# Two chunks' down projections joined into one Strassen product, with the output projection of the second chunk moved into the first one's gate and up products

## The chip, the cores and the metric

The kernel runs on one core of one Trainium2 chip. The metric is the device time of one execution in microseconds; each kernel was run several times, on the same chip as runs of the kernel before. The time is 1.7 to 2.8 us longer than the span of the trace, which goes from the first to the last instruction.

## The reference

A pre-layernorm transformer block over 2048 rows of width 1024: a sliding, dilated attention (32 heads of 32, 8 keys at distance 0, 2, ..., 14), and a bilinear feed-forward part of width 3584. Weights and rows are bf16.

```python
x = A_x
h  = x + attention(layernorm(x), wqkv) @ wo      # attention over positions s, s-2, ..., s-14
g  = layernorm(h) @ w_gate                       # (2048, 1024) @ (1024, 3584)
u  = layernorm(h) @ w_up
h2 = h + (g * u) @ w_down                        # (2048, 3584) @ (3584, 1024)
```

## The kernel before

The 2048 rows go through in four chunks of 512. TensorE first makes q, k and v of all chunks, then for chunks 0 and 1 in turn: output projection, gate and up products (7 blocks of 8 groups of 8 matmuls), down projection (chunk 1's output projection stands ahead of chunk 0's down projection). Chunks 2 and 3 are done together by a loop over pairs of blocks at the end ("the pair loop"). The attention runs on VectorE as background work: a generator whose steps are emitted between the matmul groups.

```python
# weights come in through one queue (SP) into 7 buffers; retire() frees buffers and issues the next loads
def retire(n=1):
    state["live"] -= n
    pump()

# background work: a generator yields what a step costs; ("later", us) puts it off
class Background:
    def spend(self, us): self.credit -= us          # withholds steps worth so many us
    def step(self, us): ...                         # emits steps while there is credit

def load_qk(c):                                     # q and k of chunk c for the attention, 2.1 MB
    ...
    nc.gpsimd.dma_start(qD[:], qd[c].rearrange("c g d s -> (c g) d s"))
    nc.gpsimd.dma_start(kD[:], kd[c].rearrange("c g d s -> (c g) d s"))

def attention(c):
    ...                                             # logits, Exp on ScalarE, 8 products with v
    nc.gpsimd.dma_start(od[c].rearrange("c g d s -> (c g) d s"), oD[:])        # to DRAM
    for cp in range(4):                             # and back, transposed, one row tile each
        nc.gpsimd.dma_start(oT[:, :, cp, :], od[c][cp].rearrange("(hg hl) d s -> (hl d) hg s", hl=4))

def wo_ln2(c):                                      # output projection and second layernorm, chunks 0 and 1
    def norm(t):
        ln = normalize(hs[t], mv4, rs4, t)          # VectorE
        nc.sync.dma_start_transpose(lnT[:, :, bass.ts(t, 128)], ln[:])
    ...

def ffn1(c, lnT, at={}):                            # gate and up of one chunk
    for b in range(7):
        for j in range(4):
            mm_group(pg, wts["wg", c, b], j, lnT);  nc.scalar.copy(gs[:], pg[:])
            mm_group(pu, wts["wu", c, b], j, lnT);  nc.scalar.copy(us[:], pu[:])
            nc.vector.tensor_tensor(gs[:], gs[:], us[:], ALU.mult)
            abs_sum(c, b, j)                        # ScalarE: sums of |w|, for the scales of the f16 products
            ...
        retire(2)
# ... cut: qkv, the first layernorm, the down projections, the pair loop
```

The down projection of chunk 0 was plain (224 matmuls, into `acc`), that of chunk 1 one level of Strassen (seven products of blocks, with sums and differences of blocks as operands, in f16 with power-of-two scales that come from sums of absolute values). Three words for what follows: a *total* is a matmul with ones that adds such sums over the 128 partitions, a *scale* is the power of two that VectorE makes of the total, and a *seed* is ScalarE's scaled copy of one psum bank into another, to which TensorE then adds.

## Time and profile before

| what | value |
|---|---|
| time, median of 3 runs (range) | 777.07 us (776.86 to 777.39) |
| span of the trace, granted clock | 775.2 us, 1.00 |
| TensorE busy, matmuls | 769.3 us (99%), 3691 |
| VectorE, ScalarE, GpSimd busy | 605.3, 484.0, 142.1 us |
| waits of TensorE, all together | 2.8 us: 2.2 in the start, 0.6 in the pair loop |
| bytes moved by DMA | 134.38 MB |

### The profile page before, as it was taken

To read this page: it belongs to the slowest core of one execution; us is meant where nothing else is said; L and a number is where in the kernel's file an instruction comes from. 1 tells how busy PE (TensorE), PEld (TensorE's weight loads), DVE (VectorE), ACT (ScalarE), POOL (GpSimd) and SP (SyncE) were. 2 spreads that over 40 slices of the span, in tenths; PEclk is the share of its full clock that TensorE was granted. 3 is DMA by queue.
4 is the path that set the end of the run, shared out by engine and by line. 5 is a ranking of instruction groups with operands and counts; after the bars stand their busy time and mean duration, and the time that the engine had idled before them with its cause. 6 is when DMAs were issued, how large, how long until landed. Compare 5 with 4: busy or idle time off the path is not lost.

```text
span 775.2 us, 10420 instructions
## 1 busy us (share of the span) xinstructions
PE 769.3 (99%) x3691; PEld 353.5 (46%) x3691; DVE 605.3 (78%) x766; ACT 484.0 (62%) x1040; POOL 142.1 (18%) x152
## 2 busy tenths in 40 slices
PE   8999999999999999999999999999999999999998
PEld 6444444444444444444444444444444444444444
DVE  5639999999999989999979859985553444578863
ACT  4639564322866662965777899746677776788240
POOL 0000000200002000011000001008778687600000
PEclk9999999999999999999999999999999999999999
DMA  8998896997947964978445592644332423740001
GB/s 278 265 260 199 157 230 151 299 271 224 310 133 236 308 235 125 288 257 277 142 143 192 182 299 68 157 98 114 109 95 69 109 59 106 240 140 28 0 28 55
DMA packets 183716, 134.38 MB, mean 173 GB/s; under 512 B 81264, under 2 KB 176496, under 8 KB 181616
## 3 DMA queue, kind: packets, MB, share of 16 engines
q1 hardware_dynamic: 176912, 110.12, 50.9%
q0 software_dynamic: 3584, 22.02, 8.9%
q10 hardware_dynamic: 3168, 1.57, 0.8%
q8 instruction: 29, 0.48, 0.3%
q14 instruction: 23, 0.19, 0.1%
HBM read 104.86 MB, written 22.02 MB: 164 GB/s over the span
## 4 chain that ended last, share of the span: by engine, by line
PE 93%; DVE 3%; DMA 2%; ACT 1%; issue 0%; ACTq 0%; DVEq 0%
PE ps L411 20%; PE pg L411 12%; PE pu L411 12%; PE dx L807 6%; PE pz L700 6%; PE acc L646 6%; PE py L700 6%; PE px L700 6%; PE wo L532 4%; PE wo L852 4%; PE pv L700 3%; PE dy L807 3%; PE ex L807 2%; DMA lnT<-lnr 1%; DMA w_qkv<-in_A_wqkv_dram 1%; PE ps L372 1%
## 5 line engine op out<-in xcount | busy, mean ns | idle before, releaser
L411 PE MATMUL ps<-lnT,w_qkv 128*128 128x512 bf16 x736 | 159.5, 379 | 0.0
L411 PEld LDWEIGHTS <-w_qkv 128*128 128x128 bf16 x736 | 71.9, 98 | 86.2
L411 PE MATMUL pu<-lnT,w_wu 128*128 128x512 bf16 x448 | 105.8, 379 | 0.0
L411 PE MATMUL pg<-lnT,w_wg 128*128 128x512 bf16 x448 | 105.8, 379 | 0.0
L324 ACT CAST sg<-ps 128x512 bf16<-128x512 f32 x96 | 55.2, 585 | 52.3 <-PE ps L411 49.2
L451 DVE TENSOR_TENSOR prod<-qD,kD 128x4096 bf16<-128x4096 bf16 x32 | 72.4, 2285 | 12.8 <-DMA kD<-kd 12.7
L494 DVE TENSOR_TENSOR pv<-vD,at 128x4096 bf16<-128x4096 bf16 x32 | 72.5, 2285 | 0.3
L700 PEld LDWEIGHTS <-sw 128*128 128x128 f16 x448 | 43.8, 98 | 53.8 <-issue 1.2
L411 PEld LDWEIGHTS <-w_wu 128*128 128x128 bf16 x448 | 43.8, 98 | 52.9
L411 PEld LDWEIGHTS <-w_wg 128*128 128x128 bf16 x448 | 43.7, 98 | 52.8
L616 ACT CAST us<-pu 128x512 bf16<-128x512 f32 x56 | 33.0, 590 | 43.0 <-PE pu L411 41.8
L700 PE MATMUL px<-lnT,ws 128*128 128x512 bf16 x224 | 55.2, 379 | 0.0
L700 PEld LDWEIGHTS <-ws 128*128 128x128 f16 x336 | 32.9, 98 | 39.7
L506 POOL DMA_DIRECT2D od<-oD x4 | 2.2, 542 | 264.3 <-DVE oD L504 264.3
L646 PE MATMUL acc<-w_wd,gs 128*128 128x512 bf16 x224 | 48.5, 379 | 0.0
L681 POOL TENSOR_TENSOR sw<-ws 128x512 f16<-128x512 f16 x26 | 30.0, 1152 | 85.1 <-PE py L700 77.8
L611 ACT CAST gs<-pg 128x512 bf16<-128x512 f32 x56 | 32.6, 583 | 12.9 <-PE pg L411 10.6
L453 DVE TENSOR_TENSOR prod<-prod 128x4096 bf16<-128x4096 bf16 x16 | 36.6, 2289 | 0.4
L560 ACT ACTIVATE junkd<-w_wd 128x512 bf16<-128x512 bf16 x56 | 34.3, 613 | 0.0
L646 PEld LDWEIGHTS <-gs 128*128 128x128 bf16 x224 | 21.9, 98 | 26.4
L617 DVE TENSOR_TENSOR gs<-gs,us 128x512 bf16<-128x512 bf16 x56 | 23.5, 419 | 12.5 <-ACT us L616 12.5
L185 ACT ACTIVATE rs<-mv,eps 128x1 f32<-128x1 f32 (+1 forms) x21 | 6.2, 297 | 42.0 <-DVE mv L182 36.6
(321 smaller groups left out, 1391.5 us busy)
## 6 DMA issues: line engine op xcount, KB each, us to landing
w_wg<-in_B_w_gate_dram SPq DMA_DIRECT2D x14, 1024.0 KB, 6.7
w_wu<-in_B_w_up_dram SPq DMA_DIRECT2D x14, 1024.0 KB, 5.4
w_wd<-in_B_w_down_dram SPq DMA_DIRECT2D x8, 896.0 KB, 6.2
w_pair<-in_B_w_gate_dram SPq DMA_DIRECT2D x14, 512.0 KB, 4.0
w_pair<-in_B_w_up_dram SPq DMA_DIRECT2D x14, 512.0 KB, 5.2
w_wo<-in_A_wo_dram SPq DMA_DIRECT2D x6, 1024.0 KB, 6.2
w_qkv<-in_A_wqkv_dram SPq DMA_DIRECT2D x5, 1024.0 KB, 11.0
kd<-sg SPq DMA_DIRECT2D x32, 144.0 KB, 3.3
```

The costliest lines, as they stand in the source:

```text
L324: nc.scalar.copy(sg[:, HB:HB + TC], ps[:])
L411: nc.tensor.matmul(ps[:], lhsT=wt[:, ko, bass.ts(j, 128)], rhs=rhs[:, ko, :], start=(ko == 0), stop=(ko == KO - 1))
L451: nc.vector.tensor_tensor(prod[:, j], qD[:], kD[:, :, o:o + SUB], ALU.mult)
L453: nc.vector.tensor_tensor(prod[:, :, 0:16], prod[:, :, 0:16], prod[:, :, 16:32], ALU.add)
L494: nc.vector.tensor_tensor(pv[:, j], vD[:, :, o:o + SUB], at[:, w, None, :].to_broadcast((128, DH, SUB)), ALU.mult)
L532: nc.tensor.matmul(ps[:], lhsT=oTs[c][:, kk, t, :], rhs=wts["wo", c, hf][:, kk, :], start=(kk == 0), stop=(kk == KO - 1))
L560: nc.scalar.activation(junk, src, ACTF.Abs, accum_out=self.l1[:, k:k + 1])
L611: nc.scalar.copy(gs[:], pg[:])
L616: nc.scalar.copy(us[:], pu[:])
L646: nc.tensor.matmul(acc[t][:], lhsT=hT[f][:, bass.ts(t, 128)], rhs=wts["wd", c, hf, b][:, j, :], start=(f == 0), stop=(f == NF - 1))
L700: nc.tensor.matmul(ps[:], lhsT=lhs[:, ko, :], rhs=rhs[:, ko, :], start=(fresh and ko == 0), stop=(ko == 3), skip_group_check=not fresh)
L807: nc.tensor.matmul(ps[:, bass.ds(lo, n)], lhsT=lhs[k][:, bass.ts(q, 128)], rhs=rhs[k][:, bass.ds(lo, n)], start=(fresh and k == 0), stop=( ...
```

## The change

The intent: one level of Strassen over both chunks (chunk 0 and 1 as the two row blocks of one operand) in place of a plain product and one Strassen product needs 392 matmuls in place of 420. For that, the hidden rows of both chunks must be there at once: chunk 1's go through DRAM (`hd1`), and so do the rows to which the result is added (`hsd`). The new order on TensorE is: output projection of chunk 0, gate and up of chunk 0, with the output projection of chunk 1 after the fourth of the 7 blocks; gate and up of chunk 1; output projection of chunk 2; the products A11, A12, S1, F11, F12; output projection of chunk 3; two more products; the pair loop. Two further parts: the sums of absolute values of chunk 1's products are emitted one product later than the product ("row sums one product on"), and attention steps are withheld at two places (9 us ahead of chunk 0's output projection, 6 us in the last block of chunk 1's gate and up).

```diff
@@ weights in the order of use
+    stream_wo(0)
+    for b in range(7):
+        if b == 4:
+            stream_wo(1)
+        stream_gu(0, b)
+    for b in range(7):
+        stream_gu(1, b)
+    stream_wo(2)
+    stream_down("11", 0, 0)
+    stream_down("21", 1, 0)
@@ chunk 1's second layernorm goes to ScalarE, as background work
+    class Norm2(NormOnScalar):
...
+        def transpose(self, t):
+            nc.sync.dma_start_transpose(self.lnT[:, :, bass.ts(t, 128)], self.lns[t][:])
+        def finish(self):
+            yield from self.devs()                  # 4 passes Square over 1024 elements
+            yield from self.rows()                  # 4 rows Identity over 1024, each with its transpose
+            for t in range(4):                      # the rows for the result, to DRAM
+                rows = hsd[self.c][:, t, :]
+                nc.sync.dma_start(rows, hss[self.c][t][:, D - rows.shape[-1]:D])
@@ attention
+        yield "later", 4.0 if c == 0 else 1.5
         nc.scalar.activation(lg[:], lg[:], ACTF.Exp, scale=float(DH) ** -0.5)
@@ gate and up of chunk 1: product and row sums one step later, hidden rows to DRAM
+    def ffn1_second(lnT, at):
...
+        def finish():
+            i, g, u = late.pop(0)
+            sum_last()                              # sums of the product before this one
+            nc.vector.tensor_tensor(g, g, u, ALU.mult)
...
+            done.append((i, g))
+            nc.sync.dma_start(hd1[:, bass.ts(i, 2), :], g)
...
+        for b in range(7):
...
+            if b == 6:
+                bg.spend(6.0)                       # attention steps withheld
...
@@ the order of the whole
+    bg.spend(9.0)                                   # attention steps withheld
     nxt = wo_ln2(0)
...
+    def wo_1():
+        bg.finish(sums)
+        bg.finish(atts[1])
+        n = wo_norm(1)
+        norm2.append(n)
+        norm2.append(n.finish())
+        bg.add(norm2[1], bg.now, first=True)
+    hT0 = ffn1_first(nxt[0], {4: wo_1})
+    bg.finish(norm2[1])
+    ffn1_second(norm2[0].lnT, {})
... cut: the seven products with their sums, differences and scales; the weights' sums of absolute values, now in other places and pieces; the rate of the background work, 1.02 in place of 0.98
```

## The prediction

> **What bounds the kernel now.** I read the page first: the busy shares, then the row of 40 slices.
>
> ```profile
> span 775.2 us, 10420 instructions
> ...
> PE 769.3 (99%) x3691; PEld 353.5 (46%) x3691; DVE 605.3 (78%) x766; ACT 484.0 (62%) x1040; POOL 142.1 (18%) x152
> ...
> PE   8999999999999999999999999999999999999998
> ...
> DVE  5639999999999989999979859985553444578863
> ```
>
> TensorE is busy in every slice; VectorE is nearly full from slice 4 to the middle of the run and half empty after it. So the time is the sum of the matmuls, and VectorE is the engine that could become a second bound. The list of waits of TensorE confirms it:
>
> ```profile
> PE warm_ps L318 <- DVE warm L304: 1.2, 1, 1.2
> PE pv L700 <- DVE h L812: 0.6, 2, 0.4
> PE ps L372 <- ACT lnT L367: 0.4, 1, 0.4
> PE ps L372 <- DMA w_qkv<-in_A_wqkv_dram: 0.3, 1, 0.3
> PE pt L366 <- DVE ln L359: 0.3, 1, 0.3
> ```
>
> Columns: us in total, times, longest. 2.8 us of waits in the whole run, nearly all in the start: no wait is left for the change to remove. The chain that ended last (start us, length us, what) gives the price of a matmul:
>
> ```profile
> 163.56 13.81 PE wo L532 x64
> ...
> 287.88 13.81 PE wo L532 x64
> 301.69 48.35 PE acc L646 x224
> ...
> 446.76 6.04 PE ex L807 x28
> ```
>
> 48.35/224 = 0.2158 us for each 512-column matmul. The busy time per stretch shows where VectorE has room:
>
> ```profile
> 191.20:287.90 96.70, 96.70 (x449) 43.81 (x448) 91.54 (x83) 62.63 (x117) 5.70 (x8) 1.00 0.78 249
> ...
> 350.00:446.70 96.70, 96.70 (x451) 43.84 (x449) 87.12 (x88) 73.49 (x160) 2.06 (x4) 1.00 0.57 185
> 446.70:516.80 70.10, 70.10 (x328) 31.75 (x326) 60.16 (x141) 57.23 (x76) 3.56 (x4) 1.00 0.61 164
> ```
>
> (Columns: stretch, its length, busy us of TensorE, weight loads, VectorE, ScalarE, GpSimd, granted clock, DMA share, GB/s.) In the two gate/up stretches VectorE does 91.5 and 87.1 of 96.7 us, mostly the sliding attention, which the change puts under tighter deadlines.
>
> **What the Trainium skill says.** "TensorE: Matmul & The Clock Gate", section Back-to-back issue gap, gives N/2.4 + 2.5 ns, so 216 ns at N = 512, for an isolated matmul, but 131 ns sustained. The trace has 215.8 ns in a sustained stream at clock 1.00; it agrees with the first and not with the second, so I price with 0.2158. "PSUM — Partial Sum Buffer", section Engine vs sequencer instructions: ScalarE and VectorE queues are strict FIFO. In the trace ScalarE stands 19.0 us behind four Exp that wait for VectorE; this makes the order of emission matter. "DMA: Bandwidth & Descriptors", section Issuing engines are not separate DMA queues: DMAs of all engines share 16 DMA engines. The trace agrees: the 1 MB store of the attention output took 8.2 us among weight loads and 5.3 us elsewhere. "VectorE: DVE Perf Modes", section The perf-mode tier table: a bf16 tensor_tensor runs at 2x at most, 1224 ns for 2048 elements; the trace has 1221 ns. Attention can't be made cheaper by form.
>
> **The change part by part.**
>
> Removed and added on TensorE. Before: 224 matmuls for the plain down projection of chunk 0, and 7 products x 2 row groups x 14 = 196 for chunk 1. After: one Strassen form for both, 7 x 4 x 14 = 392. The order of the built programs agrees: 7384 rows to 7328, so 56 rows, each matmul having its weight load. 28 x 0.2158 = 6.04 us saved. Two row-total matmuls become 512 columns wide instead of 64: in the timeline the next matmul follows 0.22 us later instead of 0.03, +0.38. With no new wait: 777.07 - 6.04 + 0.38 = **771.4**. That is the floor.
>
> Moved. The output projection of chunk 1 goes into the middle of chunk 0's gate/up, after block 4 of 7. Gate/up starts at 191.2, a block is 8 groups of 1.727 us = 13.81, so it is due at 191.2 + 55.3 = **246.4** instead of 287.9. When is its input there?
>
> ```profile
> 192.71 1.23 DVE L470 TENSOR_TENSOR lg<-lg,mx 128x1024 f32<-128x1024 f32 x1
> 195.06 0.69 DVE L474 TENSOR_TENSOR trs<-lg 128x512 f32<-128x512 f32 x1 [1.12 <-ACT lg L471]
> ...
> 233.59 2.28 DVE L504 TENSOR_TENSOR oD<-oD,pv 128x4096 bf16<-128x4096 bf16 x1
> ```
>
> ```profile
> 236.17 0.54 POOL L506 DMA_DIRECT2D od<-oD  x1 [62.50 <-DVE oD L504]
> 245.09 3.54 POOL L509 DMA_DIRECT2D oT<-od  x4 [8.39 <-PE pg L411]
> ```
>
> VectorE finishes chunk 1's attention at 235.9; the store lands some 8 us later, the first reload takes 3.7 us. In the new order Exp of chunk 1 stands behind the copy of the third gate/up group (due 196.4), so it ends near 198.0 and not 195.06: +2.9. The 11 products between it and the end are the same, so 195.06 + 2.9 to the end is again 40.8 us: 238.8. Store issued at 239.1; the weight loads beside it end at 241.9, so about 6 us: 245.1; first reload +0.4 + 3.7 = 249.2. TensorE waits **2.8 us**, and about 0.7 more at the second reload (before, it landed 4.5 us after the first, and one row group is 3.45 us): **3.5**.
>
> Then VectorE up to the end of chunk 3's attention, which frees the output projection of chunk 3. Before it ended at 439.9 (last add 437.61 + 2.28). Out: chunk 1's norm statistics, which go to ScalarE (8 x 0.64 + 4 x 0.15 + 4 x 0.5 = 7.7), and 8 additions of the plain down projection (8 x 0.6 = 4.8). Products of gate and up stay even (56 x 0.34 = 19.0 against 28 x 0.34 + 14 x 0.61 = 18.1). In, ahead of that last add in the queue: 8 additions of chunk 2's projection 4.8, two scales 2.3, two conversions 2.4, S1 (4096 and 3072 elements) 3.9, four results 2.7, four block conversions 4.2, four differences of 1.93 = 7.7, 25 sums of 0.34 = 8.5: 36.5. 439.9 - 7.7 - 4.8 + 36.5 = 463.9. New waits: Exp 2.9, and an estimated 1 to 4 where it stands idle for the late projection of chunk 1 or for ScalarE, which in blocks 5 to 7 gets 12 extra passes over 1024 elements (1.05 to 1.15 us each). Beside them it has per two products 4 copies of 0.48, 2 sums of 0.60 and one of about 1.94 (2048 elements, an estimate from the steps of the 512- and 1024-wide ones), 5.1 of 6.9 us; 6 x 5.1 + 13 is more than the 41.4 us of three blocks. So 467 to 471, I take 467.5.
>
> TensorE's date for that projection, in its own order: 191.2 + 96.7 (gate/up of chunk 0) + 13.8 (projection of chunk 1) + 96.7 (gate/up of chunk 1) + 14.0 (projection of chunk 2 and a total) + 5 rounds of 4 x 14 matmuls, 12.1 each (A11, A12, S1 and two more) + 0.2 = 473.1. With the 3.5 above: 476.6. Input: 467.5 + 0.3 + 5.3 (store) + 0.3 + 3.7 = 477.1. Wait: **0.5**, up to 4 if VectorE is late or the reload shares the engines with the 3.5 MB of loads queued there.
>
> Between them are two tight handovers, by my count of the queues: the scale of the down weights and the first seed (ScalarE must read a bank before TensorE adds to it), about 0.5; the first S1 product needs a difference that VectorE ends about 0.5 late; the last sums of A12 about 0.4. Together at most **1**, I count 0.5. After that the pair loop is the same, 258.4 us from its start (516.8) to the end.
>
> Sum: 771.4 + 3.5 + 0.5 + 0.5 = **775.9**, taken as 775.8.
>
> "Row sums one product on" and "steps withheld" change no count; they keep ScalarE from standing before VectorE.
>
> **The rivals.** (1) Everything hidden: 771.4. For it: the kernel is tuned, and 9 us of attention steps are withheld on purpose. Against it: the deadline moves 41 us forward, and before's own 235.9 + 8 + 4 misses it. (2) VectorE becomes the bound in the middle: if it ends 4 us later than I count, the last projection starts near 481 and the time is 779 to 781. For it: it is 95% full in the stretch. (3) The chunk 1 hidden rows now go through DRAM; 3.5 MB of reloads beside 1.8 MB of weights land near the time their conversion is due (about 420). At 330 GB/s, the rate the DMA row shows when busy, they fit; at 250 they are 4 us late, and all behind it: about 780.
>
> **Range and chances.** Lower end: the floor. Upper: rival 2 or 3 with the projection wait, 782. 2% is 15.5 us either way: faster is out of reach (the floor is 0.7% under), slower needs all rivals together.
>
> **What will show it.** Matmul count 28 lower. A wait of wo (chunk 1) for DMA oT near 246, 2 to 5 us; a second near 477, 0 to 4; waits of the A12, S1 products under 1 each. If the waits list shows neither, rival 1. If TensorE waits in A11 or A12 for a scale and VectorE for a reload of hd1, rival 3. I would be wrong altogether if the pair loop changed length.

## The result

The time went up. Ratios here are the mean time of one kernel's runs over that of the other's of the same rounds, so not quite the ratio of the medians.

| | before | after |
|---|---|---|
| time, median (range) | 776.97 us (776.84 to 777.39) | 784.62 us (782.12 to 785.09) |
| ratio, 95% interval | | 1.0091 (1.0069 to 1.0113) |
| span of the profiled run, clock | 775.2 us, 1.000 | 780.3 us, 0.996 |
| clock in the other runs | 1.000 | 0.993, 0.993, 0.996 |
| matmuls | 3691 | 3663 |

The matmuls fell by 28 as counted, and the time that they should save is gone. The profile of the changed kernel is of its fastest run. Its page (busy time and share, then slices of 19.5 us):

```profile
PE 767.6 (98%) x3663; PEld 351.8 (45%) x3663; DVE 608.2 (78%) x718; ACT 514.1 (66%) x979; POOL 142.4 (18%) x152
...
PE   9999999999999997999999999999999999999998
...
PEclk9999999999999998999999999999999999999999
```

One slice stands out, the sixteenth (293 to 312 us): TensorE is 7 tenths busy there and the granted clock is lower. The list of waits of TensorE (us in total, times, longest):

```profile
PE pwg L430 <- DMA lnT<-ln: 4.7, 1, 4.7
PE wo L574 <- DMA oT<-od: 1.9, 1, 1.9
...
PE wo L992 <- DMA oT<-od: 0.7, 1, 0.7
PE ey L641 <- DVE rowbd L636: 0.5, 1, 0.5
```

The lower three were predicted, at 3.5, 0.5 and about 0.5. The first was not: the first gate product of chunk 1 (`pwg`) waits 4.7 us for the transposes of chunk 1's second layernorm. TensorE's timeline around it (start us, length us, what, and in brackets the idle time ahead):

```profile
301.96 1.89 PE L430 MATMUL pu<-lnT,w_wu 128*128 128x512 bf16 x8
308.57 3.57 PE L430 MATMUL pwg<-lnT,w_wg 128*128 128x512 bf16 x8 [4.71 <-DMA lnT<-ln]
311.93 3.10 PE L430 MATMUL pwu<-lnT,w_wu 128*128 128x512 bf16 x8
314.87 1.89 PE L430 MATMUL pwg<-lnT,w_wg 128*128 128x512 bf16 x8
```

Eight matmuls take 1.89 us at full clock. The eight behind the wait take 3.57 and the next eight 3.10: looked at one by one, the first fourteen steps are 370 to 427 ns (twelve of them 427), then 216 again. From 308.57 to 314.65 there are 15 steps, 6.08 us in place of 15 x 0.2158 = 3.24: **2.8 us** more, while the granted clock is lower. The busy time per stretch has the clock as its third column from the right:

```profile
301.00:309.00 8.00, 3.29 (x16) 1.27 (x14) 8.00 (x8) 7.93 (x15) 0.00 (x0) 0.91 1.26 159
309.00:315.00 6.00, 6.00 (x17) 2.22 (x16) 6.00 (x4) 2.88 (x9) 0.00 (x0) 0.55 1.07 321
```

With the gaps between matmul starts (a little longer than the listed waits) the loss adds up. The pair loop starts 6.1 us later than before (522.87 against 516.8):

| from the start to the pair loop | us |
|---|---|
| 28 matmuls fewer, two wider totals | -5.7 |
| gap at the projection of chunk 1 (246 us) | +2.1 |
| gap at the first gate product of chunk 1 (303.7 us) | +4.9 |
| the matmuls at the lower clock behind it | +2.8 |
| gap between A11 and A12, waiting for scale and seed (435 us) | +1.0 |
| gap at the projection of chunk 3 (488 us) | +0.9 |
| sum | +6.0 |

The pair loop itself is 1.0 us shorter (257.4 against 258.4), which gives the 5.1 us between the spans. That 1.0 us is mostly a wait that went: before, two groups of the loop's first products wait for VectorE (0.4 and 0.2 us in the list of waits, starts together 0.97 us late, at 519.1 and 521.2); in the changed kernel the same place loses 0.1. Why the transposes were late shows in the queue of SP, which issues them (start, length of the issue, what):

```profile
279.43 5.97 SPq L556 DMA_TRANSPOSE lnT<-ln  x2
285.50 0.53 SPq L169 DMA_DIRECT2D w_wu<-in_B_w_up_dram  x1
286.08 0.63 SPq L169 DMA_DIRECT2D w_wg<-in_B_w_gate_dram  x1
286.81 15.95 SPq L556 DMA_TRANSPOSE lnT<-ln  x2
```

And in the DMA view of 284 to 310 us (what, queue, times, KB each, median us from issue to landing):

```profile
kD<-kd POOLq DMA_DIRECT2D x1, 1152.0 KB, 16.0
qD<-qd POOLq DMA_DIRECT2D x1, 1024.0 KB, 13.7
...
lnT<-ln SPq DMA_TRANSPOSE x3, 17.3
```

The first two transposes landed 3.1 us after their issue. The third, issued at 286.81, landed at 306.17, 19.4 us later; the fourth, issued at 291.22, at 308.48. TensorE wanted them at 303.7. ScalarE had the last two rows ready at 285.8 and 288.0, so they were over 15 us early. What came with them: two weight loads of 1 MB (285.50, 286.08), and the gather of q and k for chunk 3's attention (2.1 MB on GpSimd's queue, 289.19 and 289.94). The first of the weight loads could have gone at 276, when TensorE ended the fifth block and freed a buffer, the second at 282, when ScalarE had summed the last weights of another; but they stand in SP's queue behind two transposes that wait for ScalarE, which runs 4 to 7 us behind TensorE there. The gather is released by VectorE, when the last product with chunk 2's q and k has been formed; before the change that was at 275.

### The profile page after: what moved, and what is told of

Same layout as the page of the kernel before. It is cut to its first block, busy times and chain, and to the rows that moved or that the text cites. A ratio compares the mean times of both kernels' runs of the same rounds, so it can differ in the third digit from the quotient of the medians.

```text
span 780.3 us, 10300 instructions
## 1 busy us (share of the span) xinstructions
PE 767.6 (98%) x3663; PEld 351.8 (45%) x3663; DVE 608.2 (78%) x718; ACT 514.1 (66%) x979; POOL 142.4 (18%) x152
## 5 line engine op out<-in xcount | busy, mean ns | idle before, releaser
L430 PE MATMUL pwg<-lnT,w_wg 128*128 128x512 bf16 x224 | 54.6, 388 | 4.7 <-DMA lnT<-ln 4.7
L430 PE MATMUL pwu<-lnT,w_wu 128*128 128x512 bf16 x224 | 54.1, 385 | 0.0
L430 PE MATMUL pg<-lnT,w_wg 128*128 128x512 bf16 x224 | 52.9, 379 | 0.0
L430 PE MATMUL pu<-lnT,w_wu 128*128 128x512 bf16 x224 | 52.9, 379 | 0.0
L801 POOL TENSOR_TENSOR sw<-ws 128x512 f16<-128x512 f16 x26 | 29.9, 1152 | 78.6 <-PE py L820 71.3
L938 PEld LDWEIGHTS <-gs 128*128 128x128 f16 (+1 forms) x280 | 27.4, 98 | 34.0 <-issue 1.2
L837 ACT COPY py<-px 128x512 f32<-128x512 f32 x28 | 16.0, 570 | 25.5 <-PE px L820 25.5
L804 POOL TENSOR_TENSOR sw<-ws,sw 128x512 f16<-128x512 f16 x26 | 30.4, 1170 | 0.0
L802 POOL TENSOR_TENSOR sw<-sw,ws 128x512 f16<-128x512 f16 x26 | 30.0, 1155 | 2.0
L803 POOL TENSOR_TENSOR sw<-ws 128x512 f16<-128x512 f16 x26 | 30.0, 1155 | 0.0
```

Of the source, the lines that this page charges most:

```text
L430: nc.tensor.matmul(ps[:], lhsT=wt[:, ko, bass.ts(j, 128)], rhs=rhs[:, ko, :], start=(ko == 0), stop=(ko == KO - 1))
L801: eng.tensor_tensor(sw[:, i, 0], a21, a22, ALU.add)
L802: eng.tensor_tensor(sw[:, i, 1], sw[:, i, 0], a11, ALU.subtract)
L803: eng.tensor_tensor(sw[:, i, 2], a11, a21, ALU.subtract)
L804: eng.tensor_tensor(sw[:, i, 3], a12, sw[:, i, 1], ALU.subtract)
L837: nc.scalar.copy(yb[i][:], xb[i][:])
```

## The experiments

Twelve runs. The theory to be tested: three streams meet by accident (late rows on ScalarE, weight loads held up behind them, the gather), and the meeting costs 4.7 us of waiting and 3 us of clock. The rivals: each of the three alone, and a slow stretch that has nothing to do with the wait. "Clock" is the mean granted clock of the profiled run. The runs came in four sets, each on one chip and with its own runs of the kernel before (e1 to e4, e5 to e8, e9 to e11, e12); across sets the ratio is the better comparison. At a limit of 2% each of them, as the changed kernel itself, counts as the same as before, and e12 as unclear; what is read below are differences of 1 to 9 us between medians of four or five runs.

| run | what | time us (range) | ratio to before (95%) | clock |
|---|---|---|---|---|
| e1_weights_first | weight loads ahead of the transposes | 775.85 (775.61 to 777.91) | 0.999 (0.9975 to 1.0005) | 0.998 |
| e2_hold_qk | gather held until the transposes landed | 776.3 (775.7 to 776.53) | 0.9989 (0.9974 to 1.0003) | 1.000 |
| e3_fewer_sums | four weight sums fewer on ScalarE | 775.7 (775.09 to 777.11) | 0.9986 (0.9969 to 1.0003) | 1.000 |
| e4_fill | 22 idle matmuls where TensorE waits | 786.65 (785.14 to 788.2) | 1.0123 (1.0108 to 1.0138) | 0.998 |
| e5_rows_early | e1 and e2, and one scale formed earlier | 775.68 (775.26 to 780.47) | 0.9994 (0.9964 to 1.0024) | 1.000 |
| e6_no_withhold | e5, the 9 us not withheld | 777.98 (777.59 to 778.55) | 1.0008 (0.9991 to 1.0025) | 0.998 |
| e7_all | e5, 5 us withheld, one step moved | 776.66 (774.9 to 778.5) | 0.9993 (0.9974 to 1.0011) | 0.998 |
| e8_unshift | e5, row sums not put off | 781.27 (779.89 to 783.38) | 1.0054 (1.0033 to 1.0075) | 0.995 |
| e9_split_store | e5, attention output stored in four parts | 774.36 (774.03 to 775.1) | 0.9959 (0.9943 to 0.9974) | 1.000 |
| e10_best | e9, two steps of VectorE moved | 775.9 (775.57 to 776.26) | 0.998 (0.9967 to 0.9992) | 1.000 |
| e11_no_second_hold | e10, the 6 us not withheld | 780.27 (778.44 to 781.73) | 1.0035 (1.0017 to 1.0053) | 0.996 |
| e12_stall | e9, a wait put in on purpose | 793.56 (792.21 to 793.95) | 1.0205 (1.0188 to 1.0222) | 0.989 |

### e1_weights_first: the weight loads ahead of the transposes

```diff
+        held = []
         def transpose(self, t):
-            nc.sync.dma_start_transpose(...)
+            self.held.append(t)
+            if t > 1:
+                self.flush()
@@ gate and up of chunk 0, end of a block
             retire(2)
+            if b == 4:
+                norm2[0].flush()
```

> The changed kernel with one thing moved on the SP queue: the two weight loads of chunk 1's first two blocks (2 MB), which stand between the second and third layernorm transposes of chunk 1, are put ahead of all four transposes. In the changed kernel they are ready at about 276 us but are issued at 285.5 and 286.1 behind two transposes that wait for ScalarE, so that they, the q and k gather (289.2, 289.9) and the last two transposes (286.8 to 306.2, 291.2 to 308.5) share the DMA. Theory Q (the weight loads pushed into the transposes' time make them late): the last transposes land before 300, the 4.7 us wait goes, the clock is back at 1.000, and the time falls by 4.7 + 3 to 5.5 us, to 775 to 777. Theory K (the q and k gather alone makes them late): they still land at 303 or later and the time stays at 782 or more. Theory S (the rows are late on ScalarE, whatever the queue does): a wait of over 3 us stays.

SP's queue in this run:

```profile
278.09 0.37 SPq L169 DMA_DIRECT2D w_wu<-in_B_w_up_dram  x1
284.13 0.37 SPq L169 DMA_DIRECT2D w_wg<-in_B_w_gate_dram  x1
284.55 7.61 SPq L565 DMA_TRANSPOSE lnT<-ln  x4
```

The four transposes landed at 290.6, 291.5, 292.6 and 300.8; the wait at chunk 1's first gate product is not in the list any more, and the time is 775.85. One load came only at 284.13 and not at 276, since its buffer is also read by a sum on the late ScalarE. The gather still fell on the last transpose (9.9 us from issue to landing). So theory Q holds in its main point: with the weight loads ahead of the transposes, the gather alone does not make them too late. (The traced run is the slowest of the four; the others took 775.6 to 776.1 at clock 1.000. What it lost is the clock behind the wait at chunk 1's projection; see e7.)

### e2_hold_qk: the gather held back

```diff
     def load_qk(c):
         ...
+        if c == 3:
+            nc.gpsimd.tensor_copy(qD[:, 0, 0:1], norm2[0].lnT[:, 0, TC - 1:TC])   # waits for the last transpose
```

(With it, the load of chunk 3 is emitted only after the rows of the layernorm.)

> The changed kernel with the gather of chunk 3's q and k (2.2 MB, issued at 289.2 and 289.9) held until the last layernorm transpose of chunk 1 has landed, by a one-column copy on GpSimd that reads it. Attention of chunk 3 starts only after 340 us, so the hold costs nothing there. Theory K: the last two transposes land at about 296 to 299 instead of 306.2 and 308.5, the PE wait at the first gate product of chunk 1 goes, the clock is 1.000 and the time 775 to 777. Theory Q: the transposes queue behind 2 MB of weights either way and land after 302; the wait is 2 us or more and the time 779 or more. Theory S: wait of over 3 us stays, 782 or more.

The view of the transposes' tile for 275 to 315 us has this line on their times from issue to landing:

```profile
DMA to landing us min/median/max: 3.1/3.8/8.2
```

In the changed kernel the same line reads 3.1/10.2/19.4. The weight loads were issued at 285.4 and 286.0 as there, and the last transposes landed at 295.0 and 295.9, with 8.2 and 4.5 us from issue to landing. The wait is gone and the time 776.3: theory K's number came true as well. Q and K do not exclude each other, as I had put it. The traces differ in what the last two transposes meet: weight loads alone, 8.2 and 4.5 us to landing (e2); the gather alone, 9.9 for the last one (e1); both, 19.4 and 17.3 (the changed kernel). The sum of the bytes does not explain it: in e1 more than 4 MB, the second weight load, four transposes and the gather, landed between 284.1 and 300.8.

### e3_fewer_sums: ScalarE relieved

```diff
-                if j % 2:
+                if j % 2 and b not in (4, 5):
                     abs_sum("wg", b, j // 2, junk[:])
```

> The changed kernel without the four row sums of the gate weights of blocks 4 and 5 of chunk 0 on ScalarE (4 x 1.94 us; the scale of the gate and up products then comes from fewer weights, so it may be off by a power of two, not the result's meaning). Theory S (ScalarE's backlog makes the rows and with them the transposes late): the last rows end about 6 us earlier, at about 280 instead of 287.9, all transposes land before 297, the wait goes, clock 1.000, time 775 to 777. Theories Q and K: the rows come earlier but the last transposes still meet weight loads or the gather, and at least 1 us of wait stays; under K alone 780 or more.

```profile
DMA to landing us min/median/max: 3.1/10.1/20.9
```

The time is 775.7 and the wait is down to 0.6 us, but not as theory S has it. The rows came 4 us earlier, not 6, and the transposes were as slow as in the changed kernel: the last two took 20.9 and 17.0 us. They began 4 us earlier (282.58 and 287.19) and landed at 303.5 and 304.2, where TensorE's order asked for them at about 303.7 (its list has the 0.6 us there, put down to ScalarE). That is no margin; the late ScalarE decides when the three streams meet, not how long the meeting lasts.

Together: each of the three remedies alone brings back 8 to 9 us; e1 and e2 take a stream out of the meeting, e3 only moves the meeting 4 us ahead. None is "the" cause; the loss is the coincidence, late by 5 us. It is not the chip or the hour either: e4, of the same set, keeps the meeting and has the loss.

### e4_fill: idle matmuls in the wait

```diff
     bg.finish(norm2[1])
+    fill = psum.tile([128, TC], F32, tag="mm", name="fill")
+    for i in range(22):
+        nc.tensor.matmul(fill[:], lhsT=ones[:], rhs=hT0[i][:], start=True, stop=True)
     ffn1_second(norm2[0].lnT, {})
```

> The changed kernel with 22 idle matmuls (128x512, 22 x 0.2158 = 4.75 us) that nothing reads put where TensorE waits 4.7 us for the transposes. It measures the clock's share alone. If the lower granted clock after the wait costs time of its own (14 matmuls at 427 ns in place of 216 ns are 3.0 us in the profiled run, and more where the clock of the run is 0.993), the time falls by 3 to 5.5 us to 779 to 782 with the clock at 1.000. If the slow stretch had another cause (weights that arrive late, contention), the clock stays under 1 and the time stays at 784 to 785 or rises.

This one missed. The time rose to 786.65 at clock 0.998, which is what I had expected if the clock were not the wait's doing; but the run does not test that, because the wait did not go away. In the profiled run the idle matmuls filled 303.25 to 308.0 as meant, but the last transposes landed at 309.0 and 312.3, 3 to 4 us later than in the profile of the changed kernel, so that TensorE waited another 4.2 us behind them and again ran at 427 ns for a stretch; a wait of 2.1 us in the products before the pair loop came on top. Up to 303 us the two traces issue the same transposes, loads and gather, 0.4 us apart, so the landing itself varies from run to run. The run says nothing on the clock. The wait of 4.7 us in the profile of the changed kernel is of its fastest run; the others, 2.4 to 3.0 us longer, have no trace.

### e5_rows_early: both remedies, and one scale earlier

In e1 and e2 TensorE waits 1.8 to 1.9 us for the last row of the down weights' sums (0.5 in the changed kernel, where everything was late anyway). VectorE forms it behind a conversion that waits for a reload.

```diff
             conv_h1(a21, 0)
+            scale_d.rows()
             conv_h1(a22, 0)
             s1_half(0)
-            scale_d.rows()
```

> Both remedies together (weight loads ahead of the transposes, q and k gather of chunk 3 held) and one more step: on VectorE the last row of the sums for the down weights' scale is formed before the second conversion of reloaded hidden rows, which waits for its reload, not after it. In the two runs with one remedy TensorE waits 1.8 to 1.9 us there; the sums it needs are ready at 420.2, it asks at 423.5. Theory: that wait goes to 0, the others stay (projection of chunk 1: 2.0, of chunk 3: 0.8), clock 1.000: 774.0 to 775.0. Rival (the conversion and the scale are then late elsewhere): the wait moves to the next products and the time stays at 775.5 to 776.5.

The rival won. The list now has no wait for that row, and one of 1.9 us for ScalarE's seed at the first A12 product: the scale is formed at 428.25 as before, because VectorE copies the total out only behind two more steps of 2.3 us each. The time of 775.68 lies in the rival's range. One of the four runs took 780.47 (clock 0.998), the others 775.3 to 776.0; that run has no trace.

### e6_no_withhold and e11_no_second_hold: the withheld steps undone

```diff
-    bg.spend(9.0)
     nxt = wo_ln2(0)
```

> The same as the run before in this set, with one part of the change undone: the 9 us of attention steps withheld ahead of chunk 0's output projection. Theory A (the steps withheld are what makes chunk 1's attention late by the time its projection is due): the 2.0 us wait at chunk 1's projection goes and the time falls by up to 2 us to 772 to 773. Theory B (the steps withheld keep VectorE free for chunk 0's layernorm): a wait of 1 to 4 us comes in at the first gate product of chunk 0 (about 191 us) and the time is 775 to 778.

Both theories missed in what they name; the time, 777.98, is theory B's by another way. The store of chunk 1's attention went out 2.8 us earlier (236.46), but landed at 244.07, as ever, and the wait at the projection of chunk 1 stayed, 2.2 us. No wait came at chunk 0's gate. Instead ScalarE stood more at other places, and TensorE waits 2.7 us for the total of chunk 1's sums at 412:

```profile
ACT lg L500 <- DVE lg L498: 9.3, 1, 9.3
```

(This is ScalarE's list of waits from 300 to 414 us; in e5 the same line reads 4.0.) The time is 2.3 us longer than e5's. The second place, in the version e10:

```diff
-            if b == 6:
-                bg.spend(6.0)
```

> e10_best with a part of the change undone: the 6 us of attention steps withheld in the last block of chunk 1's gate and up products. Theory A (they keep VectorE free for the sums that gate the first down products): without them a wait of 1 to 3 us comes at the scale of chunk 1's hidden rows or at the first A12 product, 773 to 776. Theory B (they only order what VectorE has time for): within 0.5 us of e10_best.

Theory A, and more than it allowed: 780.27 against 775.9. ScalarE's list there has a wait for one product of VectorE at the very end of chunk 1's gate and up, which is not in e10's list:

```profile
ACT ring L646 <- DVE ring L762: 4.0, 1, 4.0
```

and TensorE waits 3.4 us for the total behind it. Half clock for 6.8 us, from within that wait on, is part of the loss. So both places of withholding are worth something, 2.3 and 4.4 us, and neither shows as a count.

### e7_all: less withheld, one step moved

```diff
-    bg.spend(9.0)
+    bg.spend(5.0)
@@ A12 products
-            t_half(b11, b12, b11, q - 1) if q < 3 else None
+            t_half(b11, b12, b11, q - 1) if q < 3 else pull(1)
```

> Candidate for the best version: the first of this set, with 5 us of steps withheld instead of 9 and one step of chunk 3's attention moved from the products before its projection into the A12 products, where VectorE has about 4 us free by my count. Theory: both projection waits (2.0 and 0.8 us) shrink to under 0.5 each; 771.5 to 773.0, with 771.4 the floor by the count of matmuls. Rival (VectorE is full there, a step moved only moves the wait): 774 to 775.5.

The wait at the projection of chunk 3 went as expected, but the time, 776.66, is above both ranges. The wait at the projection of chunk 1 stayed at 2.0: the store was issued at 236.64 and landed at 244.32. Three of the four runs have a clock of 0.997 or 0.998. The stretch 250 to 256 us, right behind the 2.0 us wait, in this run and then in e5:

```profile
250.00:256.00 6.00, 6.00 (x22) 2.40 (x21) 2.47 (x4) 1.19 (x4) 0.00 (x0) 0.77 1.07 318
```

```profile
250.00:256.00 6.00, 6.00 (x30) 2.70 (x29) 5.41 (x7) 1.15 (x2) 0.00 (x0) 1.00 1.08 325
```

After the same wait one run has a clock of 0.77 and 22 matmuls in these 6 us, the other 1.00 and 30. This looks like chance, but the traces' records of the clock show more. The start and the end of a run aside, every stretch of half clock is 3.41 us long or a multiple of it, and within one execution all changes of the clock lie on one raster of 3.41 us. In e7 the 2.0 us of standing fall whole into one step of the raster (245.98 to 249.39), and the next step is at half clock:

```profile
245.98:249.39 3.41, 1.40 (x8) 0.43 (x7) 3.38 (x5) 2.42 (x3) 3.13 (x4) 1.00 0.66 170
249.40:252.81 3.41, 3.41 (x10) 1.21 (x9) 1.32 (x2) 0.78 (x3) 0.00 (x0) 0.50 1.06 309
252.82:256.23 3.41, 3.41 (x17) 1.54 (x16) 1.97 (x3) 1.15 (x2) 0.00 (x0) 1.00 1.06 322
```

In e8 (below) TensorE stands 3.36 us ahead of 414.09, but a border of the raster lies inside, 1.5 and 1.9 us, and the clock stays whole:

```profile
408.78:412.19 3.41, 1.95 (x10) 0.69 (x7) 3.41 (x4) 2.36 (x5) 0.00 (x0) 1.00 0.41 114
412.19:415.60 3.41, 1.51 (x7) 0.70 (x8) 3.38 (x6) 3.41 (x8) 0.00 (x0) 1.00 1.06 344
415.60:419.01 3.41, 3.41 (x17) 1.57 (x16) 3.31 (x9) 3.41 (x9) 0.00 (x0) 1.00 1.09 349
```

In all traces that show such changes in mid-run (the changed kernel, e1, e4, e6, e7, e8, e11, e12), half clock followed each of the nine steps with 2.01 us of standing or more (as the list of waits counts it) and none with 1.94 or less, where the clock was whole before. So what counts is the standing inside one step, and with it where the wait happens to fall. One step at half clock costs a busy TensorE 1.7 us (an estimate, half of 3.41), which is part of the spread of these kernels. e5's trace has no record of a change, so where its raster lay is not shown.

### e8_unshift: the row sums not put off

```diff
             done.append((i, g))
+            sum_last()
             nc.sync.dma_start(hd1[:, bass.ts(i, 2), :], g)
```

> The first of this set with another part of the change undone: the row sums of chunk 1's products come right behind their product on ScalarE again, not one product on. ScalarE then stands up to 0.6 us at each of 14 sums until VectorE has multiplied. Theory (as the prediction has it, no count changes, only standing): TensorE is not held, because the psum buffers give it several groups of room: within 0.5 us of the first of this set. Rival: ScalarE, 66% busy and late here, falls behind and holds TensorE's psum buffers: 1 to 4 us longer, with waits of chunk 1's gate products on ScalarE.

The rival, beyond its range: 781.27, 5.6 us over e5. ScalarE's list of waits from 300 to 424 us:

```profile
ACT ring L645 <- DVE ring L761: 26.6, 13, 3.7
```

It stands 26.6 us for VectorE's products at 13 of the 14 sums (in e5: not in the list), is behind at the end of chunk 1, and TensorE waits 3.4 us for the total of these sums and 2.8 for the seed of A12, with half clock behind the second (and behind the 2.0 us at chunk 1's projection). My "up to 0.6 us at each sum" took VectorE to be free; it has a 2.3 us attention step in its queue nearly always.

### e9_split_store: four stores in place of one

```diff
-        nc.gpsimd.dma_start(od[c].rearrange("c g d s -> (c g) d s"), oD[:])
+        for cp in range(4):
+            nc.gpsimd.dma_start(od[c][cp], oD[bass.ts(cp, 32)])
```

> As e5_rows_early, with the store of each chunk's attention output (1 MB, issued at 239.3 and landed at 244.0 for chunk 1) cut into four stores of 256 KB, so that the first reload waits for its own quarter only. In the two runs that ended chunk 1's attention 2.7 us earlier (stores issued at 236.5 and 236.6) the one store still landed at 244.1 and 244.3 and the wait stayed 2.0 to 2.2 us: the store, beside 2 MB of weights, sets it. Theory: the first reload lands near 246 instead of 248.6, the 2.0 us wait at chunk 1's projection falls under 0.5, and the 0.8 us wait at chunk 3's goes; 773.0 to 774.0, and no run with a lowered clock after 246 us. Rival (the DMA is full there and four stores take as long as one): the wait stays over 1.5 us, 775 to 776.

The first quarter was stored by 242.7, and the first reload landed at 247.8, not at 246: less than hoped, since the reload itself took 4.6 us beside the other stores. The wait fell from 2.1 to 0.7, that at the projection of chunk 3 went, and no run shows a lowered clock. So the theory holds, with both its numbers (under 0.5, 773 to 774) missed by a little:

```profile
PE ex L955 <- ACT ey L1078: 1.7, 1, 1.7
...
PE ez L955 <- DVE hsr L795: 1.2, 1, 1.2
PE wo L589 <- DMA oT<-od: 0.7, 1, 0.7
```

774.36 us is the best time here, 0.4% under the kernel before by the ratio and 1.3% under the changed kernel by the medians.

### e10_best: two steps moved on VectorE

```diff
             conv_h1(a22, 0)
-            s1_half(0)
         if q == 1:
-            pull(1)
             ...
             for i in range(3):
                 seed(i)
+            s1_half(0)
+            pull(1)
```

> Candidate for the best version: e9_split_store with one attention step and one sum of reloaded rows moved on VectorE behind the forming of the down weights' scale. In e5_rows_early that scale came at 428.25, behind 2.3 + 2.2 us of those two, and TensorE waited 1.9 us at the first A12 product; ScalarE is busy until 426.7 in any case, so I expect 0.3 us of that wait left. 771.5 to 772.8 against 775.7 for e5_rows_early; the count of matmuls puts the floor at 771.4. Rival (VectorE is full from here to chunk 3's projection, so what is put off comes back as a longer wait there): 773.5 to 775.5 with a wait of over 1.5 us at chunk 3's projection or in the products before it.

The label promised too much; the rival holds. The 1.7 us wait at A12 went, and a larger one came at the next product, whose operand (a difference of weights) is now late:

```profile
PE ev L955 <- DVE w_dn L948: 2.4, 2, 1.5
```

The time is 775.9, 1.5 us over e9. VectorE has no room in this stretch: what is put off comes back as a wait of the same order.

### e12_stall: a wait put in on purpose

```diff
     bg.finish(norm2[1])
+    hold = lnp.tile([128, 1024], BF, tag="ln", name="hold")
+    for i in range(3):
+        nc.gpsimd.tensor_tensor(hold[:, bass.ts(i % 2, 512)], hT0[27][:], hT0[26][:], ALU.add)
+    fill = psum.tile([128, TC], F32, tag="mm", name="fill")
+    nc.tensor.matmul(fill[:], lhsT=ones[:], rhs=hold[:, 0:512], start=True, stop=True)
     ffn1_second(norm2[0].lnT, {})
```

> The fastest version so far (e9_split_store: no wait of over 2 us, clock 1.000 in all four runs, 774.4) with a wait of TensorE put in on purpose where the changed kernel has one, ahead of chunk 1's first gate product: one idle matmul there needs the last of three additions on GpSimd (1.15 us each) of chunk 0's last hidden row, so that TensorE stands about 5 us. It measures what such a wait costs beside its own length, without late transposes. Theory (the lower granted clock comes from TensorE's standing): behind the wait some 10 to 25 matmuls take 427 ns each in place of 216, the run's clock is 0.993 to 0.997, and the time rises by the wait plus 2 to 5.5 us, to 781 to 785. Rival (the slow stretch of the changed kernel came of late weights or a full DMA, and waiting costs its own length only): clock 1.000 and 779 to 780.

The wait came out three times as long as meant (VectorE multiplied the last row only at 308.9, and the additions on GpSimd took 5.3, 3.2 and 1.1 us), so the numbers for the total do not apply. What it was built for it shows:

```profile
319.05 0.58 PE L931 MATMUL fill<-hold,ones 128*128 128x512 bf16 x1 [16.59 <-POOL hold L929]
319.43 3.62 PE L430 MATMUL pwg<-lnT,w_wg 128*128 128x512 bf16 x8
322.84 2.46 PE L430 MATMUL pwu<-lnT,w_wu 128*128 128x512 bf16 x8
```

Behind the wait the matmuls are 427 ns apart from 319.4 to 323.7, 5.0 us for 12 steps in place of 2.6: 2.4 us. The run is 19.2 us longer than e9; the gap (16.7) and the slow stretch (2.4) make 19.1. The weights and transposes had long landed, and the DMA share in 312 to 330 us was 0.02. So the slow stretch comes of TensorE's standing and not of late data. In the same place e9, which does not wait there, has full clock throughout.

## Why the prediction was right or wrong

The predicted 775.8 with a range from the floor (771.4) to 782 was too low by 8.8 us; the measured median lies 2.6 us above the range.

- **Floor of 771.4: held.** 28 matmuls fewer, at the predicted price. The waits and the clock account for the rest to 0.1 us up to the pair loop.
- **Chunk 1's projection, 3.5 us: right place and mechanism, too large.** It was due at 246.3 (predicted 246.4), VectorE ended at 238.9 (238.8), the store was issued at 239.2, the first reload landed at 248.4 (249.2): a gap of 2.1 us. The additional 0.7 for the second reload did not come (by the prediction's own numbers, 4.5 - 3.45, it would have been 1.0).
- **VectorE's later course and the projection of chunk 3, 0.5 us: held.** (The terms add up to 467.8 to 470.8, so the 467.5 that was taken lies below its own sum; in e5 the last store was issued at 466.8.) In e5, where nothing else disturbs, TensorE came to it at 477.3 (predicted 476.6), and the first reload had landed at 476.7 (477.1). The wait, 0.7 to 0.9, came at the second reload and not at the first.
- **Handovers, 0.5 us: too small by half.** 1.0 us in the changed kernel, about 1.9 in e1 and e2.
- **Rival 1 (all hidden): wrong.** Rival 2 (VectorE ends late): no. Rival 3 (reload of chunk 1's rows): the waits named for it, in A11 and A12, were under 1 us in the changed kernel. Its sign did show in e1 and e2: VectorE waits 2.1 us for a reload of chunk 1's rows, and TensorE 1.9 and 1.8 us for the scale behind it. The time stayed near 776, not 780.
- **The step that failed.** The prediction saw that ScalarE gets 12 passes more and that "6 x 5.1 + 13 is more than the 41.4 us of three blocks", but used it only as a delay of VectorE. It gave no date at all to the one thing that these passes make: chunk 1's transposed rows, due at 191.2 + 96.7 + 13.8 = 301.7 plus the waits. ScalarE's lateness alone would have been harmless: the last row was ready at 288.0, a transpose without company lands in 3.1 us, and TensorE came at 303.7, 12 us later. But in its queue SP holds the weight loads behind the transposes, and the gather is released by VectorE at just that time. The prediction cites that all DMAs share 16 engines, and applied it to the stores of the attention, not to these transposes. What the runs show in its place: the last two transposes landed at 306.2 and 308.5, 17 to 19 us after their issue in place of 3.1, and TensorE stood 4.9 us for them in the profiled run; e1, e2 and e3 each take that wait away or down to 0.6 us.
- **A term that was not in the sum: the clock.** It had no line for what TensorE's clock does after a wait: 2.8 us in the profiled run. The Trainium skill has it, on the page that the prediction cites ("TensorE: Matmul & The Clock Gate", Part 1, sections What's actually happening and, for the last figure, Wait — 56ns, not 53.3ns?): after an idle window of about 3.4 us the array runs at half clock until it has been busy for about as long, and N = 512 matmuls are then 426.7 ns apart. The traces agree on the 427 ns and on the busy time until full clock: 5.8 us in the changed kernel, 4.9 in e12, 3.4 in e7; on the idle time see the last section. With this page read for that, a risk of a 4 us wait should have been priced at about 6 (an estimate from the page: some 3.4 us at half clock lose 1.7; measured here, 4.9 and 2.8).
- **"They keep ScalarE from standing before VectorE": right, and without a number.** In e8, e6 and e11 this is worth 5.6, 2.3 and 4.4 us.
- **"Wrong altogether if the pair loop changed length":** it is 1.0 us shorter, since its two waits for VectorE went. The prediction had put nearly all of the 2.8 us of waits in the start, and so saw none that the change could remove; 0.6 us of the list stood here.

With any one of the three remedies, the sum of the prediction is what is measured: 775.7 to 776.3 against 775.8. That is partly luck, since the projection of chunk 1 costs less and the handovers more than it said.

Still open: what the 2.4 to 3.0 us between the profiled run of the changed kernel and its other runs are (by their mean clocks, 0.996 and twice 0.993, two of the three had one step of half clock more, at most 1.7 us, and one had none, so most of it is likely waiting; an estimate, no trace); what made one of e5's runs 780.47; and why the DMA moved only 239 GB/s in 285 to 306 us in the changed kernel, with its engines nearly full, against 302 and 313 GB/s in e1 and e2 (the mix of transposes, gather and weights differs; no run isolates it).

## What to carry to other kernels

When work is moved, give a date to everything that gates the first instruction behind it, transfers included, and list what else is issued in the 10 us before that date: each queue may be in time alone and the three together late. A queue that issues loads in order couples engines that have nothing to do with each other, so loads that are ready belong ahead of transfers that wait for a late engine. On a kernel bound by TensorE, price every possible wait with the clock behind it, and cut a store whose first part is wanted first.

## What the Trainium skill lacked or had wrong

- "TensorE: Matmul & The Clock Gate", section HAM oscillation, gives as its rule no idle gaps of over about 3.4 us. Here 2.0 us were enough when they fell into one step of the clock's raster (e7: 2.01 of 3.41 us, then half clock), while 1.94 us in one step (the changed kernel) and 3.36 us over two steps (e8) left the clock whole. The page's 426.7 ns is borne out, and so is its note that the number of slow matmuls varies from run to run with the place in the window.
- No page gives the time from issue to landing of a DMA transpose of 128 x 1024 bf16, alone or beside other transfers. It was 3.1 us alone, 4.5 to 9.9 us beside weights or a gather (e2, e1), and 17.0 to 22.7 us beside both, 2 MB of weights and a 2.1 MB gather issued within 5 us (the changed kernel, e3, e4).
- "SBUF — State Buffer", section Who interferes with whom, says that a VectorE instruction with two SBUF inputs contends with a GpSimd instruction that reads SBUF. The runs agree and add a size: additions of 128 x 512 bf16 on GpSimd took 5.3 and 3.2 us beside VectorE's 128 x 4096 products, and 1.1 us for the last one (e12).
